# Retention and SiLU feed-forward on one core: the first two slices of w_in loaded first in 2 KB rows, TensorE given matmuls to do until data lands, the early order rewritten

## The chip, the cores and the metric

The kernel runs on one core of a Trainium2 chip. The metric is the device time of one execution in microseconds, lower being better. The version before has a median of 623.32 us over four runs (620.6 to 625.35). The profiled execution is one of them.

## The reference, cut to what matters

The computation has two parts. The first is a decayed linear recurrence over time for 4 batches and 8 heads, with sequence length 768 and head dimension 64. The second is a feed-forward layer with SiLU over the 3072 rows that come out of it.

```python
state = zeros((B, H, D, D))
for t in range(S):
    state = gamma[None, :, None, None] * state + einsum('bhd,bhe->bhde', k[:, :, t], v[:, :, t])
    y[:, :, t] = scale * einsum('bhd,bhde->bhe', q[:, :, t], state)
x = y.transpose(0, 2, 1, 3).reshape(B * S, H * D)      # 3072 x 512
h = x @ w_in                                           # 512 x 2048
out = (h / (1 + exp(-h))) @ w_out                      # 2048 x 512
```

q, k and v arrive as 32-bit floats. The two weight matrices arrive as 64-bit floats.

## The kernel before, in words

**Units.** The sequence is cut into 6 chunks of 128 steps. A unit is one chunk of one batch, so there are 24 units, numbered chunk by chunk; units 0 to 3 are chunk 0. For a unit n, in the names of the order written out at the end of the kernel:

- `T(n)` transposes k and q on TensorE (4 transposes each, L436), and ScalarE copies each result from PSUM (L438). k's result goes to a PSUM bank that `turn` hands out, q's to another.
- `K(n)` scales k by powers of the decay on VectorE (L398); `Q(n)` does it for the transposed q (L403).
- `SC(n)` is 16 matmuls for the new state's sums (L452) and 16 for the scores (L462). `A(n)` has three steps: the mask, which multiplies the scores by the decay on VectorE (L470), then the middle state (L476 on ScalarE in chunk 0, L478 on VectorE later), then the new state (L482).
- `YA(n)` and `YB(n)` multiply the masked scores and the states into y (L501). Between them a one-element memset on GpSimd (L377) keeps two groups of matmuls on PSUM in order.
- `X(n)` has four steps in chunks 0 and 1: ScalarE copies y from PSUM to SBUF (`ys`, L542); ScalarE writes the high part of x (L557); VectorE the low part (L560); VectorE a third part (L563). The parts exist because each feed-forward product is done as three products of a reduced 32-bit float type.

**Slices of w_in.** The feed-forward layer's hidden dimension is cut into 16 slices of 128. `W(i)` does the next of eleven steps that turn slice i's 64-bit words into three parts. In order: 1 absolute value (ScalarE, L196); 2 sign (L199); 3 clamp (L202); 4 shift and join (L206); 5 exponent (L209); 6 low words times a factor (L212); 7 sum (L217), all these on VectorE; 8 high part (ScalarE, L120); 9 remainder (VectorE, L123); 10 middle part (ScalarE, L126); 11 third part (VectorE, L128). A slice is 512 KB, loaded by three DMAs in rows of 1 KB (`load_w`, L178 and L180), into one of two staging buffers.

**Products.** `P(n)` is the first product of 12 matmuls (L650) for one chunk and one slice: eight into `ha`, four into `hb`. The eight need the slice's high and middle parts and x's high and low parts for all four units of the chunk. `CL(n)` closes it in three steps: copy (L660), subtraction on VectorE (L665), SiLU (L670). Results go to memory (`put_g`, L676), and a second half of the kernel multiplies them by w_out (L967).

**Order.** Every engine works through its instructions in the order in which the program issues them. Up to L882 the order of all engines is written out by hand (L768 to L881); later a loop over products runs the rest of the units behind the products. SyncE's queue first takes loads of k, q and v for units 0 to 5 with the first two slices between them (after unit 0 and after unit 3), each load 256 KB in rows of 256 bytes. Then come slice 2 and the loads of further units, in the order of the calls.

The bounds of the parts in the order before: units 0 to 3 run with W(0) and some of W(1) between them; then `P(0)` (L818), unit 4 and the rest of W(1), three steps of W(2), `T(6)`, and `P(1)` (L835).

Of the kernel before, what the change touches and what calls it, by code (L numbers as in the profile page):

```python
# [33 lines left out]
def kernel(  # L34
# [39 lines left out]
    wide = moe_w_in.dtype == mybir.dt.int64  # L74

    scale = 1.0 / math.sqrt(D)
# [8 lines left out]
    wpool = pool("wpool", 1)  # L85
# [3 lines left out]
    one = pool("one", 1)  # L89
    hpool = pool("hpool", 3)  # L90
    stage = pool("stage", 2)
    conv = pool("conv", 1)
# [46 lines left out]
    kqv = {"k": {}, "q": {}, "v": {}}  # L139
    EARLY = 2 * B  # L140
# [21 lines left out]


    staged = {}

    def load_w(i):
        if i >= 2 * NF:
            return
        if wide:
            t = stage.tile([128, 2 * DM], U32, tag="wf", name=f"wf_{i}")  # L170
            w_in, w_out, n = moe_w_in.bitcast(U32), moe_w_out.bitcast(U32), 256
        else:
            t = stage.tile([128, DM], FP32, tag="wf", name=f"wf_{i}")
            w_in, w_out, n = moe_w_in, moe_w_out, 128
        if i < NF:
            to = t.rearrange("p (i o f) -> o p i f", o=2, f=n)
            src = w_in[:, ts(i, n)].rearrange("(i o p) f -> o p i f", o=2, p=128)
            nc.sync.dma_start(out=to[0], in_=src[0])  # L178
            for j in range(2):
                nc.sync.dma_start(out=to[1, ts(j, D)], in_=src[1, ts(1 - j, D)])  # L180
        else:
            nc.sync.dma_start(out=t, in_=w_out[ts(i - NF, 128), :])
        staged[i] = t

    def convert_steps(i, out):

        t = staged.pop(i)
        if not wide:
            out.append(t)
            return  # L190
        words = t.rearrange("p (c w) -> p c w", w=2)
        lo, hi = words[:, :, 0], words[:, :, 1]
        p = a = conv.tile([128, DM], U32, tag="ca", name=f"ca_{i}")
        s = conv.tile([128, DM], U32, tag="cs", name=f"cs_{i}")
        with queue(evac[0] if evac else None):
            nc.scalar.activation(out=a.bitcast(FP32), in_=hi.bitcast(FP32), func=AF.Abs,  # L196
                                 scale=65536.0)
        yield
        nc.vector.tensor_scalar(out=s, in0=hi, scalar1=0x80000000, scalar2=None,  # L199
                                op0=ALU.bitwise_and)  # L200
        yield
        nc.vector.tensor_scalar(out=a.bitcast(FP32), in0=a.bitcast(FP32),  # L202
                                scalar1=bits(1024 << 20), scalar2=bits((1279 << 20) - 1),
                                op0=ALU.max, op1=ALU.min)
        yield
        nc.vector.scalar_tensor_tensor(out=s, in0=a, scalar=3, in1=s,  # L206
                                       op0=ALU.logical_shift_left, op1=ALU.bitwise_or)
        yield
        nc.vector.tensor_scalar(out=p, in0=s, scalar1=0xFF800000, scalar2=None,  # L209
                                op0=ALU.bitwise_and)  # L210
        yield
        nc.vector.scalar_tensor_tensor(out=p.bitcast(FP32), in0=lo, scalar=2.0 ** -52,  # L212
                                       in1=p.bitcast(FP32), op0=ALU.mult, op1=ALU.mult)
        yield
        w = (s.bitcast(FP32) if i < NF else
             conv.tile([128, DM], FP32, tag="cw", name=f"cw_{i}"))
        nc.vector.tensor_tensor(out=w, in0=s.bitcast(FP32), in1=p.bitcast(FP32), op=ALU.add)  # L217
        out.append(w)
# [68 lines left out]
    def begin_w():  # L287
# [10 lines left out]
    early_order.enter_context(tc.manual_schedule(engines={  # L298
        mybir.EngineType.SP, mybir.EngineType.DVE, mybir.EngineType.Activation,
        mybir.EngineType.Pool}))  # L300
    for n in range(EARLY - 2):
        for name in "kqv":
            load(name, n)
        if n in (0, 3):
            load_w(n // 3)


    ident = const.tile([128, 128], FP32, tag="ident", name="ident")
# [10 lines left out]
    for j in range(2):  # L319
        for a in range(HP):  # L320
            nc.scalar.activation(out=decay[:, j, a, :], in_=lag[:, :D], func=AF.Exp,
                                 scale=float(lg[2 * a + j]))
# [40 lines left out]
    def banks(tag, name, n=2):  # L363
        return ps_u.tile([128, n, 512], FP32, tag=tag, name=name)
# [3 lines left out]
    def turn(name):  # L368
        turns[0] += 1
        return ps_h.tile([128, 512], FP32, tag=f"h{turns[0] % 3}", name=name)  # L370
# [55 lines left out]
        nc.scalar.copy(out=to[n].bitcast(U16).rearrange("p a (t w) -> p w a t", w=2),  # L426
                       in_=turned.pop((name, n)).rearrange("p (w a) t -> p w a t", w=2))

    def stage_t(n):

        for name, to, bufs, src, tp in (
                ("kt", kt, 2, kqv["k"][n], turn(f"kp_{n}")),
                ("qt", qt, 3, kqv["q"].pop(n), banks("q", f"qp_{n}", 1)[:, 0])):
            tp = tp.rearrange("p (a t) -> p a t", a=HP)
            for a in range(HP):
                nc.tensor.transpose(tp[:, a, :], src[:, 2 * a : 2 * a + 2, :], ident)  # L436
            to[n] = one.tile([128, HP, C], FP32, tag=name, name=f"{name}_{n}", bufs=bufs)
            evac[:] = [nc.scalar.copy(out=to[n], in_=tp).ins]  # L438

    def score_tile(n):  # L440
        u = banks("s", f"sc_{n}")
# [85 lines left out]
    def finish_y(n, yp):  # L527
        list(steps_y(n, yp))

    raws = []  # L530

    def steps_y(n, yp):
        c, b = units[n]
        if b == 0:
            p, tag = (wpool, "wq") if c == LATE else (xpool, "xt")
            xt[c] = p.tile([128, 3, KIN, NT], FP32R, tag=tag, name=f"xt_{c}")
        raw = None
        if c < LATE:
            if n == 0:
                raws.append(wpool.tile([128, LATE * B, KIN, C], FP32, tag="wq", name="ys"))  # L540
            raw = raws[0][:, n]
            nc.scalar.copy(out=raw.rearrange("p a (o t) -> p o a t", o=2), in_=yp)  # L542
        elif c == LATE:
            raw = hpool.tile([128, KIN, C], FP32, tag="hs", name=f"ys_{n}")
            nc.scalar.copy(out=raw.rearrange("p a (o t) -> p o a t", o=2), in_=yp)
            nc.sync.dma_start(out=y_dram[b], in_=raw)
        yield from split_x(c, b, yp, raw)
# [125 lines left out]
    def put_g(keep):  # L673
        while len(pending) > keep:
            c, f, g = pending.pop(0)
            nc.sync.dma_start(out=g_dram[c, f], in_=g)  # L676
# [50 lines left out]

    sa, ys, asteps, ysteps = {}, {}, {}, {}

    def T(n):  # L730
        stage_t(n)

    def SC(n):
        sa[n] = sc, sums = score_tile(n)
        stage_s(n, sums)
        stage_a(n, sc)
        asteps[n] = steps_a(n, sc, sums)

    def A(n):
        next(asteps[n], None)  # L740

    def YA(n):
        ys[n] = stage_y(n)
# [12 lines left out]
    def W(i, times=1):  # L756
        if i not in slices:
            slices[i] = early_slice(i)
        for _ in range(times):
            next(slices[i], None)  # L760

    def loads(n):
        for name in "kqv":
            load(name, n)

    K, Q = scale_k, scale_q

    T(0), K(0)  # L768
    nc.scalar.activation(out=token, in_=lgc[:1, :1], func=AF.Silu)
    SC(0), A(0), Q(0), A(0), A(0)  # L770
    W(0), W(0), W(0), W(0), W(0)
    YA(0), YB(0), X(0)
    T(1), K(1)
    W(0)
    load_w(2)
    W(0)
    X(0), X(0)
    SC(1), A(1)
    W(0)
    A(1)  # L780
    Q(1), A(1)
    T(2), K(2)
    W(0), X(0)
    W(0), W(0)
    YA(1), SC(2)
    A(2)
    YB(1), X(1)
    A(2), Q(2), A(2)
    X(1)
    T(3), K(3)  # L790
    X(1), X(1)
    YA(2), YB(2), X(2)
    SC(3), A(3), A(3), Q(3), A(3)
    X(2), W(1), W(1)
    X(2), X(2)
    YA(3), YB(3), X(3), X(3)
    W(1), W(1)
    T(4)
    X(3), X(3)
    K(4)  # L800
    W(1), W(1)
    loads(EARLY - 2), loads(EARLY - 1)
    closing = {}

    def P(n):
        c, f = divmod(n, NF)
        closing[n] = close_steps(c, f, *multiply(c, f))

    def CL(f):
        next(closing[f], None)  # L810

    def KA(n):
        t = kqv["k"][n]
        for h in range(H):
            nc.scalar.activation(out=t[:, h, :], in_=t[:, h, :], func=AF.Copy,
                                 scale=gk[:, units[n][0], h : h + 1])

    P(0)  # L818
    next_chunk()
    SC(4)  # L820
    CL(0), CL(0), CL(0)
    put_g(0)
    W(1)
    T(5)
    A(4), A(4), Q(4), K(5), A(4)
    W(1), W(1)
    YA(4), SC(5), YB(4)
    loads(EARLY)
    load_w(3)
    W(2), W(1)  # L830
    A(5)
    W(1), W(2), W(2)
    X(4)
    T(6)
    P(1)  # L835
    A(5), Q(5), A(5)
    KA(6)
    W(2), W(2), W(2)
    load("k", EARLY + 1), load("q", EARLY + 1)
    load_w(4)  # L840
    W(2)
    CL(1), CL(1)
# [184 lines left out]
```

## Time and profile before

| | us |
|---|---|
| median of four runs | 623.32 |
| the profiled execution, whole | 622.53 |
| its span, first to last instruction | 620.7 |
| TensorE busy (matmul rows) | 601.8 |
| VectorE busy | 423.4 |
| ScalarE busy | 312.7 |

The time of a run is the span and some 1.8 us around it. Times of instructions are counted from the span's start. In the profile a 32-bit float matmul has two rows, one for each pass: the scores are 384 matmuls and have 768 rows; a transpose has one row. "Granted clock" is the share of full speed that TensorE's clock gate gave.

The beginning is where the change is:

| stretch, us | TensorE busy | VectorE busy | ScalarE busy | DMA, GB/s |
|---|---|---|---|---|
| 0 to 5 | 0.80 | 0.00 | 3.96 | 137 |
| 5 to 10 | 4.05 | 2.10 | 3.84 | 239 |
| 10 to 15 | 3.38 | 4.90 | 2.98 | 200 |
| 15 to 20 | 3.67 | 4.79 | 3.72 | 212 |
| 20 to 25 | 3.45 | 3.15 | 2.26 | 195 |
| 25 to 30 | 2.91 | 3.87 | 3.14 | 216 |
| 30 to 35 | 5.00 | 3.37 | 2.04 | 227 |
| 35 to 40 | 4.24 | 4.28 | 4.04 | 254 |

### The profile page before, as it was taken

Reading aid. Unit: us, or ns where it says so; the run is one execution under the profiler, and the core shown is the slowest. Engines: PE = TensorE matmul, PEld = TensorE weight load, DVE = VectorE, ACT = ScalarE, POOL = GpSimd, SP = SyncE. Lnnn points to the kernel's source line nnn. Section 1 sums busy time; section 2 is a strip of 40 time slices with the busy share of each in tenths; the row PEclk is TensorE's granted clock in tenths of the full one; section 3 lists DMA queues with packets and bytes.
Section 4 is the critical chain, followed back from the end, with each engine's and each line's share of the span. In section 5 each row is a group of like instructions: output and inputs, shape, how many; then the busy total and the mean of one; then the engine's idle time right before and its main releaser. Section 6 shows DMA issues by size and latency. Waiting matters only on the chain.

```text
span 620.7 us, 13494 instructions
## 1 busy us (share of the span) xinstructions
PE 601.8 (97%) x5384; PEld 496.1 (80%) x5384; DVE 423.4 (68%) x731; ACT 312.7 (50%) x595; POOL 22.5 (4%) x79
## 2 busy tenths in 40 slices
PE   5799999999999999999999999999999999999997
PEld 4577787888888888888788888888888888888886
DVE  4889899898889877767599783644635454554631
ACT  7668797666655666666588741412222221412311
POOL 3000000000001211111000000000000000000000
PEclk9999999999999999999999999999999999999999
DMA  9998896555567899989767552432523433442301
GB/s 189 218 224 193 217 243 205 178 171 194 201 159 234 242 253 227 259 223 295 260 220 255 203 150 72 149 123 75 187 79 120 152 101 103 136 135 83 122 1 68
DMA packets 137998, 107.31 MB, mean 173 GB/s; under 512 B 94800, under 2 KB 103248, under 8 KB 137936
## 3 DMA queue, kind: packets, MB, share of 16 engines
q1 hardware_dynamic: 135056, 101.21, 57.7%
q10 hardware_dynamic: 2880, 5.24, 2.3%
q8 instruction: 42, 0.69, 0.5%
q14 instruction: 20, 0.16, 0.1%
HBM read 66.06 MB, written 36.70 MB: 166 GB/s over the span
## 4 chain that ended last, share of the span: by engine, by line
PE 83%; DVE 0%; DVEq 0%; issue 0%; POOLq 0%
PE ha L650 25%; PE o L967 21%; PE oa L967 14%; PE hb L650 12%; PE ob L967 7%; PE y L501 2%; PE sc L462 1%; PE sc L452 1%; PE o L975 0%; PE oa L975 0%; PE qp L436 0%; PE kp L436 0%; PE ob L975 0%; DVE o L993 0%; DVEq L1022 0%
## 5 line engine op out<-in xcount | busy, mean ns | idle before, releaser
L650 PE MATMUL ha<-xt,wi 128*128 128x512 f32 x768 | 195.2, 396 | 1.1 <-ACT xt L557 0.7
L650 PEld LDWEIGHTS ha<-xt,wi 128*128 128x128 f32 x768 | 143.0, 189 | 33.3 <-ACT wi L126 1.2
L967 PE MATMUL o<-wo,gs 128*128 128x512 f32 x564 | 143.2, 389 | 0.0
L717 DVE TENSOR_TENSOR gs<-gr,gs 128x512 fp32r<-128x512 f32 x96 | 62.3, 686 | 90.2 <-ACT gs L715 90.2
L967 PEld LDWEIGHTS o<-wo,gs 128*128 128x128 f32 x564 | 105.9, 188 | 21.8
L715 ACT ACTIVATE gs<-gr 128x512 fp32r<-128x512 f32 x96 | 53.6, 621 | 134.2 <-issue 131.8
L967 PE MATMUL oa<-wo,gs 128*128 128x512 f32 x376 | 115.9, 390 | 0.0
L650 PE MATMUL hb<-xt,wi 128*128 128x512 f32 x384 | 102.9, 390 | 0.7 <-DVE g L665 0.7
L665 DVE TENSOR_TENSOR g<-g,hb 128x512 f32<-128x512 f32 x96 | 65.8, 685 | 43.6 <-ACT g L660 25.0
L650 PEld LDWEIGHTS hb<-xt,wi 128*128 128x128 f32 x384 | 72.1, 188 | 16.1 <-DVE g L665 1.1
L670 ACT ACTIVATE g<-g 128x512 f32<-128x512 f32 x96 | 60.3, 628 | 46.9 <-DVE g L665 46.8
L967 PEld LDWEIGHTS oa<-wo,gs 128*128 128x128 f32 x376 | 70.6, 188 | 14.8
L967 PE MATMUL ob<-wo,gs 128*128 128x512 f32 x188 | 73.8, 392 | 0.0
L660 ACT ACTIVATE g<-ha 128x512 f32<-128x512 f32 x96 | 57.0, 593 | 31.9 <-PE ha L650 18.2
L718 DVE SCALAR_TENSOR_TENSOR gs<-gs 128x512 fp32r<-128x512 f32 x96 | 62.1, 685 | 0.0
L967 PEld LDWEIGHTS ob<-wo,gs 128*128 128x128 f32 x188 | 35.3, 188 | 8.6 <-DVE o L985 1.6
L196 ACT ACTIVATE ca<-wf 128x512 f32<-128x512 f32 x32 | 21.4, 667 | 7.0 <-DVE cw L217 5.8
L212 DVE SCALAR_TENSOR_TENSOR ca<-wf,ca 128x512 f32<-128x512 uint32 x32 | 22.8, 711 | 0.5
L984 ACT ACTIVATE o<-o 128x512 f32<-128x512 f32 x10 | 6.0, 599 | 33.4 <-PE o L967 33.0
L206 DVE SCALAR_TENSOR_TENSOR cs<-ca,cs 128x512 uint32<-128x512 uint32 x32 | 22.1, 692 | 0.9
L470 DVE TENSOR_TENSOR am<-sc,decay 128x512 f32<-128x512 f32 x24 | 16.5, 688 | 8.3 <-PE sc L462 8.2
L501 PE MATMUL y<-qt,mid 64*64 64x64 f32 x384 | 19.7, 220 | 2.3 <-issue 1.8
(93 smaller groups left out, 556.6 us busy)
## 6 DMA issues: line engine op xcount, KB each, us to landing
gd<-g SPq DMA_DIRECT2D x96, 256.0 KB, 3.2
gr<-gd SPq DMA_DIRECT2D x96, 256.0 KB, 2.7
wf<-in_moe_w_out_dram SPq DMA_DIRECT2D x16, 512.0 KB, 4.4
out_dram<-o ACTq DMA_DIRECT2D x20, 256.0 KB, 2.1
wf<-in_moe_w_in_dram SPq DMA_DIRECT2D x16, 256.0 KB, 4.0
wf<-in_moe_w_in_dram SPq DMA_DIRECT2D x32, 128.0 KB, 3.9
kf<-in_k_dram SPq DMA_DIRECT2D x16, 256.0 KB, 5.2
qf<-in_q_dram SPq DMA_DIRECT2D x16, 256.0 KB, 4.3
```

The source lines that it names most:

```text
L196: nc.scalar.activation(out=a.bitcast(FP32), in_=hi.bitcast(FP32), func=AF.Abs, scale=65536.0)
L206: nc.vector.scalar_tensor_tensor(out=s, in0=a, scalar=3, in1=s, op0=ALU.logical_shift_left, op1=ALU.bitwise_or)
L212: nc.vector.scalar_tensor_tensor(out=p.bitcast(FP32), in0=lo, scalar=2.0 ** -52, in1=p.bitcast(FP32), op0=ALU.mult, op1=ALU.mult)
L501: i = nc.tensor.matmul(yp[ts(e, D), o, a, :], lhsT=lhsT, rhs=rhs, start=(e, o) not in started, stop=True, skip_group_check=True).ins
L650: nc.tensor.matmul(hb if i == 2 else ha, lhsT=w_sb[f][:, i, ts(kk, 128)], rhs=xt[c][:, i, kk, :], start=kk == 0 and i != 1, stop=kk == KIN ...
L660: copied[:] = [nc.scalar.activation(out=hs, in_=ha, func=AF.Copy, scale=ONE_E).ins]
L665: taken_out[:] = [nc.vector.tensor_tensor(out=hs, in0=hs, in1=hb, op=ALU.subtract).ins]
L670: nc.scalar.activation(out=hs, in_=hs, func=AF.Silu)
L715: nc.scalar.activation(out=t[:, 0, :], in_=g, func=AF.Copy, scale=HALF)
L717: nc.vector.tensor_tensor(out=t[:, 1, :], in0=g, in1=high, op=ALU.subtract)
L718: nc.vector.scalar_tensor_tensor(out=t[:, 2, :], in0=t[:, 1, :].bitcast(FP32), scalar=-1.0 / EPS, in1=high, op0=ALU.mult, op1=ALU.add)
L967: nc.tensor.matmul(o, lhsT=g, rhs=wo[f][:, i, :], start=f == 0 and i != 1, stop=f == NF - 1 and i != 0)
```

## The change

Four things are edited.

1. **Loads.** A new function `load_pair` loads slices 0 and 1 together, ahead of all loads of k, q and v, in three DMAs (512 KB and twice 256 KB) whose rows are 2 KB. They land in a tile `room` that takes the place of the tile `ys` in the same memory. Slice 0's two scratch tiles lie in `room` as well, so W(0) and W(1) no longer share scratch. The bytes are the same. Slice 2 no longer waits for a staging buffer. The loads of k and q for unit 9 are issued ahead of slice 3 in place of behind it.
2. **x of units 0 to 3.** Their y is no longer copied to SBUF: the high part (ScalarE) and the low part (VectorE) of x are read from PSUM. The first step of `X(n)` does nothing for these units. Units 4 to 7 keep the copy.
3. **TensorE.** A new function `keep_busy` issues 22 matmuls of the identity by itself ahead of `T(0)`.
4. **The order by hand** up to `P(1)`: the steps of W(0) and W(1) begin ahead of unit 0; `T(n)` of units 1 to 4 is cut into its k and its q half with `YA` between; masks stand ahead of the x steps of the unit before; `SC(4)` stands ahead of `P(0)`. From `P(1)` on the order of compute is unchanged.

```diff
+    room = [wpool.tile([128, 12 * DM], U32, tag="wq", name="room")]
+
+    def load_pair():
+        ...
+        t = room[0][:, 8 * DM :].rearrange("p (r f) -> p r f", f=2 * 256)
+        to = t.rearrange("p (i o) f -> o p i f", o=2)
+        src = moe_w_in.bitcast(U32)[:, : 2 * 256].rearrange("(i o p) f -> o p i f", o=2, p=128)
+        nc.sync.dma_start(out=to[0], in_=src[0])
+        for j in range(2):
+            nc.sync.dma_start(out=to[1, ts(j, D)], in_=src[1, ts(1 - j, D)])
+        for i in range(2):
+            staged[i] = t[:, :, ts(i, 256)]
...
+    load_pair()
     for n in range(EARLY - 2):
         for name in "kqv":
             load(name, n)
-        if n in (0, 3):
-            load_w(n // 3)
...
+    def keep_busy(n, t=None):
+        t = turn(f"none_{turns[0]}") if t is None else t
+        for _ in range(n):
+            nc.tensor.matmul(t[:, :128], lhsT=ident, rhs=ident, start=True, stop=True)
+        return t
...
-        if c < LATE:
-            if n == 0:
-                raws.append(wpool.tile([128, LATE * B, KIN, C], FP32, tag="wq", name="ys"))
-            raw = raws[0][:, n]
+        if B <= n < LATE * B:
+            raw = room[0][:, ts(n - B, DM)].bitcast(FP32).rearrange("p (a t) -> p a t", a=KIN)
             nc.scalar.copy(out=raw.rearrange("p a (o t) -> p o a t", o=2), in_=yp)
...
+    keep_busy(22)
+    nc.scalar.activation(out=token, in_=lgc[:1, :1], func=AF.Silu)
+    W(0, 2), W(1, 2)
+    W(0, 3)
+    load_w(2)
     T(0), K(0)
...
+    W(0, 3), W(1)
+    SC(0)
     W(0)
+    A(0), A(0), Q(0), A(0)
+    T(1, "k"), K(1)
+    W(0)
+    YA(0), T(1, "q"), YB(0)
     W(0)
     X(0), X(0)
+    SC(1)
+    X(0), W(1)
+    A(1), A(1), Q(1)
+    T(2, "k")
+    A(1), K(2), X(0)
+    YA(1), T(2, "q"), YB(1), X(1), X(1)
+    SC(2)
+    X(1), W(1)
+    A(2), A(2), Q(2)
+    T(3, "k")
+    A(2), K(3), X(1)
+    YA(2), T(3, "q"), YB(2), X(2), X(2)
+    SC(3)
+    X(2)
+    A(3), A(3), Q(3)
+    T(4, "k")
+    A(3), K(4), X(2)
+    YA(3), T(4, "q"), YB(3), X(3), X(3)
+    SC(4)
+    X(3)
+    A(4), X(3)
     loads(EARLY - 2), loads(EARLY - 1)
...
+    next_chunk()
     P(0)
-    next_chunk()
-    SC(4)
-    CL(0), CL(0), CL(0)
+    A(4), Q(4), A(4)
+    W(1)
+    CL(0)
+    T(5)
+    CL(0), CL(0)
     put_g(0)
+    W(1, 2)
+    K(5)
+    YA(4), SC(5), YB(4)
+    W(1, 2)
+    A(5)
     W(1)
-    T(5)
-    A(4), A(4), Q(4), K(5), A(4)
-    W(1), W(1)
-    YA(4), SC(5), YB(4)
     loads(EARLY)
+    load("k", EARLY + 1), load("q", EARLY + 1)
     load_w(3)
-    W(2), W(1)
-    A(5)
-    W(1), W(2), W(2)
+    W(2, 3)
     X(4)
     T(6)
     P(1)
```

More of the change, by code (lines that the diff above doesn't have):

```diff
@@ L164 @@
     staged = {}
+    room = [wpool.tile([128, 12 * DM], U32, tag="wq", name="room")]
+    def load_pair():
+        if not wide:
+            load_w(0), load_w(1)
+            return
+        t = room[0][:, 8 * DM :].rearrange("p (r f) -> p r f", f=2 * 256)
[6 more added lines that the diff above has]
+            staged[i] = t[:, :, ts(i, 256)]
     def load_w(i):
@@ L190, in convert_steps, with by_rows @@
             return
[L191 to L194, printed above, removed]
+        if len(t.shape) == 2:
+            t = t.rearrange("p (r f) -> p r f", r=KIN)
+        words = t.rearrange("p r (c w) -> p r c w", w=2)
+        lo, hi = words[:, :, :, 0], words[:, :, :, 1]
+        def by_rows(x):
+            return x.rearrange("p (r c) -> p r c", r=KIN)
+        if i == 0:
+            p = a = room[0][:, ts(4, DM)]
+            s = room[0][:, ts(5, DM)]
+        else:
+            p = a = conv.tile([128, DM], U32, tag="ca", name=f"ca_{i}")
+            s = conv.tile([128, DM], U32, tag="cs", name=f"cs_{i}")
         with queue(evac[0] if evac else None):
-            nc.scalar.activation(out=a.bitcast(FP32), in_=hi.bitcast(FP32), func=AF.Abs,
-                                 scale=65536.0)
+            nc.scalar.activation(out=by_rows(a.bitcast(FP32)), in_=hi.bitcast(FP32),
+                                 func=AF.Abs, scale=65536.0)
         yield
-        nc.vector.tensor_scalar(out=s, in0=hi, scalar1=0x80000000, scalar2=None,
+        nc.vector.tensor_scalar(out=by_rows(s), in0=hi, scalar1=0x80000000, scalar2=None,
                                 op0=ALU.bitwise_and)
@@ L211, in convert_steps @@
         yield
-        nc.vector.scalar_tensor_tensor(out=p.bitcast(FP32), in0=lo, scalar=2.0 ** -52,
-                                       in1=p.bitcast(FP32), op0=ALU.mult, op1=ALU.mult)
+        nc.vector.scalar_tensor_tensor(out=by_rows(p.bitcast(FP32)), in0=lo,
+                                       scalar=2.0 ** -52, in1=by_rows(p.bitcast(FP32)),
+                                       op0=ALU.mult, op1=ALU.mult)
         yield
@@ L427, in join_t, with stage_t @@
                        in_=turned.pop((name, n)).rearrange("p (w a) t -> p w a t", w=2))
[L429 to L433, printed above, removed]
+    def stage_t(n, names="kq"):
+        for name in names:
+            if name == "k":
+                to, bufs, src, tp = kt, 2, kqv["k"][n], turn(f"kp_{n}")
+            else:
+                to, bufs, src, tp = qt, 3, kqv["q"].pop(n), banks("q", f"qp_{n}", 1)[:, 0]
             tp = tp.rearrange("p (a t) -> p a t", a=HP)
@@ L436, in stage_t @@
                 nc.tensor.transpose(tp[:, a, :], src[:, 2 * a : 2 * a + 2, :], ident)
-            to[n] = one.tile([128, HP, C], FP32, tag=name, name=f"{name}_{n}", bufs=bufs)
+            to[n] = one.tile([128, HP, C], FP32, tag=f"{name}t", name=f"{name}t_{n}", bufs=bufs)
             evac[:] = [nc.scalar.copy(out=to[n], in_=tp).ins]
+    def keep_busy(n, t=None):
[3 more added lines that the diff above has]
+        return t
     def score_tile(n):
@@ L528, in finish_y @@
         list(steps_y(n, yp))
-    raws = []
     def steps_y(n, yp):
@@ L728, with T @@
     sa, ys, asteps, ysteps = {}, {}, {}, {}
-    def T(n):
-        stage_t(n)
+    def T(n, names="kq"):
+        stage_t(n, names)
     def SC(n):
@@ L766 @@
     K, Q = scale_k, scale_q
-    T(0), K(0)
[L769 to L773, printed above, removed]
-    W(0)
-    load_w(2)
+    keep_busy(22)
[3 more added lines that the diff above has]
+    load_w(2)
+    T(0), K(0)
+    W(0, 3), W(1)
+    SC(0)
+    W(0)
+    A(0), A(0), Q(0), A(0)
+    T(1, "k"), K(1)
+    W(0)
+    YA(0), T(1, "q"), YB(0)
     W(0)
     X(0), X(0)
[L778 to L796, printed above, removed]
-    W(1), W(1)
[L798 to L801, printed above, removed]
+    SC(1)
[19 more added lines that the diff above has]
+    A(4), X(3)
     loads(EARLY - 2), loads(EARLY - 1)
@@ L816, in KA @@
                                  scale=gk[:, units[n][0], h : h + 1])
+    next_chunk()
     P(0)
-    next_chunk()
-    SC(4)
-    CL(0), CL(0), CL(0)
-    put_g(0)
-    W(1)
-    T(5)
-    A(4), A(4), Q(4), K(5), A(4)
-    W(1), W(1)
-    YA(4), SC(5), YB(4)
+    A(4), Q(4), A(4)
[3 more added lines that the diff above has]
+    CL(0), CL(0)
+    put_g(0)
+    W(1, 2)
[3 more added lines that the diff above has]
+    A(5)
+    W(1)
     loads(EARLY)
+    load("k", EARLY + 1), load("q", EARLY + 1)
     load_w(3)
-    W(2), W(1)
-    A(5)
-    W(1), W(2), W(2)
+    W(2, 3)
     X(4)
@@ L838 @@
     W(2), W(2), W(2)
-    load("k", EARLY + 1), load("q", EARLY + 1)
     load_w(4)
```

## The prediction, made before the change had run

> **What bounds the kernel now.** I read first the page's busy shares and the chain of work that ended last, then that chain in order of time.
>
> ```profile
> PE 601.8 (97%) x5384; PEld 496.1 (80%) x5384; DVE 423.4 (68%) x731; ACT 312.7 (50%) x595; POOL 22.5 (4%) x79
> ...
> PE 83%; DVE 0%; DVEq 0%; issue 0%; POOLq 0%
> ...
> 100.26 0.04 issue
> 100.31 1.20 PE ha L650 x4
> ```
>
> From 100.3 us to the end the chain is TensorE alone. The change can only bring that stretch forward: before 100 us TensorE is busy 85.3 us (sum of the windows), so 14.7 us are idle there, nearly all before 60 us. Next, windows; the columns are busy time of PE, PEld, DVE, ACT and POOL, then granted clock, DMA share and GB/s.
>
> ```profile
> 21.95:25.36 3.41, 2.31 (x112) 2.06 (x112) 1.84 (x5) 1.81 (x4) 0.04 (x1) 1.00 1.20 231
> 25.36:28.78 3.42, 1.51 (x17) 1.33 (x17) 2.32 (x5) 1.56 (x4) 0.04 (x1) 0.98 0.92 198
> 28.78:32.19 3.41, 3.41 (x8) 2.71 (x9) 2.95 (x5) 2.04 (x6) 0.00 (x0) 0.52 0.91 242
> ...
> 38.48:63.51 25.03, 23.60 (x528) 19.16 (x519) 23.48 (x44) 19.80 (x50) 0.35 (x4) 1.00 0.87 206
> ```
>
> From 38.48, where unit 5's mask starts, VectorE is busy 23.48 of 25.03 us. Its order from there on is nearly the same after the change, so **what counts is when unit 5's mask starts** (38.48 now): whatever it gains or loses is carried into the TensorE-bound part. The VectorE and TensorE timelines show what delays it:
>
> ```profile
> 8.49 0.69 DVE L470 TENSOR_TENSOR am<-sc,decay 128x512 f32<-128x512 f32 x1 [2.41 <-PE sc L462]
> ...
> 23.41 0.69 DVE L470 TENSOR_TENSOR am<-sc,decay 128x512 f32<-128x512 f32 x1 [1.71 <-PE sc L462]
> ...
> 33.40 0.69 DVE L665 TENSOR_TENSOR g<-g,hb 128x512 f32<-128x512 f32 x1 [1.60 <-PE hb L650]
> ...
> 38.48 0.69 DVE L470 TENSOR_TENSOR am<-sc,decay 128x512 f32<-128x512 f32 x1 [0.72 <-PE sc L462]
> ```
>
> ```profile
> 20.06 0.68 PE L501 MATMUL y<-am,kqv 64*64 64x64 f32 x26
> 21.10 0.34 PE L501 MATMUL y<-am,kqv 64*64 64x64 f32 x6 [0.36 <-issue]
> ...
> 26.95 0.45 PE L501 MATMUL y<-qt,mid 64*64 64x64 f32 x8 [1.77 <-issue]
> ...
> 28.74 3.63 PE L650 MATMUL ha<-xt,wi 128*128 128x512 f32 x8 [0.32 <-ACT xt L557]
> ```
>
> VectorE starves behind TensorE. TensorE has three troubles: late data, stalls that wait for nothing shown ("issue"), and a halved clock in P(0).
>
> **The stalls are instruction fetch.** Counting matmul rows in program order (T 8, SC 64, YA 40, YB 8 for a unit of chunk 0), the stalls at 21.10 and 25.46 to 26.95 fall at rows 346 and 473: 127 apart, with their weight loads some 256 instructions. The DMA view shows one 16 KB packet of the instruction queue from 12.4, 18.6, 23.8, 29.2 and 37.8 us, each 2 to 3 us after TensorE passes row 92, 219, 346, 473 or 600:
>
> ```profile
> q8 instruction: 1, 0.02, 41.2%
> ```
>
> That is the one of 12.4 to 12.6: 41.2% of 16 engines for 0.2 us is 1.32 us on one of them. So passing one edge fetches the block behind the next. Row 219 passes at 16.45, 346 at 21.10, 473 at 26.95: **4.65 and 5.85 us per block of 127 rows, mean 5.25**.
>
> **The change, part by part.**
>
> **Loads.** Issue plus time to landing, per DMA: k0 4.05, q0 5.3, v0 6.4, slice 0 8.7, k1 9.8, q2 15.6, q3 19.4, v3 21.5, slice 1 24.1, v4 27.4. A k, q or v takes 1.2 us each undisturbed and (21.5 - 9.8)/8 = 1.46 us on the average; slices take 2.3 and 2.6. Both first: the link effectively starts at 4.05 - 1.2 = 2.85, so the pair lands at 2.85 + 4.9 = 7.75 at the rate of 1 KB rows, or at 6.35 at the 303 GB/s of the fastest early microsecond; 2 KB rows have no row here. I take 6.6, nearer the fast end since rows are longer. Then k0 7.8, q0 9.0, v0 10.2, k1 11.4, and at 1.46: v1 14.3, v2 18.7, v3 23.1, v4 27.4. Unit 0 gets its data 3.8 us later, unit 4 at the same time. Slice 0 is 2.1 us and slice 1 17.5 us earlier. The k and q moved past slice 3 are needed at 55; slice 3 at 59.6: nothing.
>
> **VectorE and ScalarE.** Up to unit 5's mask VectorE issues about 31 instructions of 512 elements at a 0.60 us pitch and 18 short ones at 0.34: 25 us. From 6.6 that fits by 31.6, so VectorE no longer decides unless TensorE is much faster. Four copies of 0.59 us (L542) go; ScalarE is not the bound here: nothing. Instead low parts are read from PSUM (0.69, by L470 and L665, which read PSUM and take the same) and hold y's bank some 1.3 us longer; the next YA comes a mask later: nothing, or 0.6 us per unit if masks come early. Silu's table load (1.28) moves behind gq, 5.5 to 6.8, under the pair's transfer; it can hold slice 0's first step by 0.4 us.
>
> **keep_busy.** 22 f32 matmuls are 44 rows; nearest are the k transposes of the same shape: cold 4 in 1.09 us, pitch 0.21, later 4 in 0.66, pitch 0.13. From 1.4 us (identity ready at 1.31): 16 cold rows to 4.9, where the clock would open, 28 at 0.13: done at 8.5; if it opens only at 8.3, at 9.8. So T(0) starts 0.7 (at most 2.0) after k0, but warm: T(0) and SC(0) take 2.2 us less than the cold 4.2 to 8.43, 0.4 us each for four groups being the visible part. I take SC(0) at 10.3 to 11.5, against 6.5 to 8.4.
>
> **The TensorE chain with fetch.** Rows in the new order: SC(0) ends at 116, SC(1) 236, SC(2) 356, SC(3) 476, SC(4) 596, P(0) 608, SC(5) 728; each 44 later for the keep_busy, and P(0) also 64 for SC(4). Row 92 passes at 10.9, so 219 (in SC(1), data at 14.3) opens at 16.15, 346 (in SC(2)) at 21.4, 473 (end of SC(3)) at 26.65, 600 at 31.9. After 473: mask and T(4) of k to 27.5, YA(3) 28.4, T(4) of q 29.0, YB(3) 29.4, SC(4) 30.6, P(0) 30.7 to 34.1 with 0.6 lost at row 600. T(5) 1.1, YA(4) 0.9: SC(5) starts 36.1, and unit 5's mask 1.2 later (as now): **37.4, a gain of 1.1 us**. P(0) starts 2 us later than now, but at full clock and with unit 4's scores done.
>
> **Two rules against the rows.** Row: stalls of 0.4 and 1.5 us at block edges. The Trainium skill, "Runtime: NRT & Kernel Launch", Instruction fetch mechanics, says that crossing a 16 KiB boundary is "mostly hidden". By it nothing but data decides: SC(4) at v4, P(0) at 28.5, T(5) 31.5, unit 5's mask at 34.8, a gain of 3.7. I keep the row. Row: the clock halved at 28.78 after a window with 1.51 of 3.42 us busy and no gap over 1.77; 1.98 busy (11.71 to 15.12) didn't halve it. The skill's "TensorE: Matmul & The Clock Gate", Part 1, puts the fall after at least one idle window, which by its text would never come here. By the row I expect about 2.1 busy in that window after the change: kept, though barely; if not, P(0) loses 1.6 us as now (3.63 + 1.09 against 2.09 + 1.07 for P(1)).
>
> **Sum.** Against this execution: 622.5 - 1.1 = **621.4 us**. It stands 0.8 below the median of 623.3. A difference under 0.5% (3.1 us) can't be told from none.
>
> **Rivals.**
> - **Fetch hides, or is quick (30%).** For: the stalls come only with fully loaded queues, at 33 to 39 us there are none. Against: the load is the same. At 4.65 us per block the mask starts near 36.0: 620.0; all hidden: 618.8.
> - **Slower: unit 0's lateness is not made up (20%).** Its place is SC(0), 3.8 us later, with 44 rows more ahead of each SC. For: blocks at 5.85 us give edges 16.75, 22.6, 28.45, 34.3, P(0) at 32.5 to 36.3, mask at 40.2: a loss of 1.7; the window to 28.78 is then nearly idle, the clock halves, 1.0 more: 625.2. It decides once a block takes over 5.5 us. Against: only one did.
> - **It does not do what it says (5%).** keep_busy leaves a gap to k0, the clock falls again, and SC(0) runs cold: 0.9 later, about 622.3.
>
> The forecast holds 45%. Range 617.8 to 625.6: both first rivals' ends with 1 us below and 0.4 above. Faster by over 0.5% needs most of the hidden fetch or a gain I have not found: 0.31; slower by as much needs more than the slow rival: 0.18; else 0.51.
>
> **What would show it.** Right: the pair landed by 6.6; SC(0) near 10.3 and warm; "issue" stalls in SC(1) to SC(3) at 127-row distances; P(0) 30 to 31 at clock 1.0; unit 5's mask near 37.4. Wrong: no such stalls; P(0) before 28.7; clock 0.5 in P(0); VectorE idle between 40 and 63.

## The result, and the profile after

The changed kernel takes **623.73 us** (median of 35 runs, 621.62 to 628.18), the kernel before 623.03 in the runs beside it. The ratio is 1.0018, 95% interval 1.0005 to 1.0031: slower by about a fifth of a per cent, where 621.4 had been forecast. The profiled execution took 623.75 us with a span of 621.9, against 622.53 and 620.7 before.

The busy shares and the chain of work that ended last:

```profile
PE 607.3 (98%) x5428; PEld 501.3 (81%) x5428; DVE 423.2 (68%) x731; ACT 310.8 (50%) x591; POOL 22.0 (4%) x79
...
PE 83%; issue 0%; DVE 0%; DVEq 0%; POOLq 0%
```

The chain still ends in a long TensorE stretch. TensorE is busy 5.5 us more: the 44 rows of keep_busy take 7.8, and P(0) at full clock takes less. The only difference in its list is that "issue" now stands second. Next, the windows that answer to those of before (busy time of PE, PEld, DVE, ACT and POOL, then granted clock, DMA share and GB/s), and VectorE's and TensorE's timelines of the early part:

```profile
21.90:25.30 3.40, 3.16 (x96) 2.58 (x96) 3.11 (x7) 1.50 (x4) 0.09 (x1) 1.00 0.74 168
25.30:28.70 3.40, 2.45 (x87) 1.87 (x80) 2.24 (x5) 1.30 (x3) 0.00 (x0) 1.00 0.82 184
28.70:32.10 3.40, 3.40 (x83) 2.90 (x84) 2.80 (x5) 2.25 (x6) 0.09 (x1) 1.00 0.94 231
37.24:62.27 25.03, 23.14 (x528) 18.90 (x529) 23.38 (x44) 20.90 (x52) 0.35 (x4) 1.00 0.91 216
```

```profile
7.86 0.43 DVE L222 TENSOR_SCALAR room<-room 128x512 uint32<-128x512 uint32 x1 [7.86 <-DMA room<-in_moe_w_in_dram]
...
37.24 0.69 DVE L501 TENSOR_TENSOR am<-sc,decay 128x512 f32<-128x512 f32 x1 [0.27 <-PE sc L493]
```

```profile
1.37 7.80 PE L468 MATMUL none<-ident 128*128 128x128 f32 x44 [1.37 <-POOL ident masks.py:199]
...
11.23 0.69 PE L483 MATMUL sc<-kqv 64*64 64x64 f32 x32 [0.65 <-DMA kqv<-in_v_dram]
...
21.94 0.34 PE L493 MATMUL sc<-qt,kt 64*64 64x64 f32 x8 [0.41 <-issue]
26.74 0.21 PE L493 MATMUL sc<-qt,kt 64*64 64x64 f32 x1 [0.75 <-issue]
30.55 2.12 PE L677 MATMUL ha<-xt,wi 128*128 128x512 f32 x8
```

So far the forecast holds in the main: SC(0) at 11.23 and warm, stalls in SC(2) and SC(3) at rows 348 and 475 (127 apart), P(0) at 30.55 with the clock at 1.00, unit 5's mask at 37.24. (The stall forecast in SC(1) did not come.) The mask is 1.24 us earlier than in the trace of before. Followed on, that lead is 0.85 us at VectorE's tenth subtraction of `CL`, which closes a product; here it is in the change, then before:

```profile
87.28 0.68 DVE L692 TENSOR_TENSOR g<-g,hb 128x512 f32<-128x512 f32 x1
```

```profile
88.13 0.68 DVE L665 TENSOR_TENSOR g<-g,hb 128x512 f32<-128x512 f32 x1
```

The lead is still 0.82 at 192 us, and a loss of 1.2 at the end. TensorE's timeline of the change between 190 and 204 us shows where it turns:

```profile
192.35 0.96 PE L677 MATMUL ha<-xt,wi 128*128 128x512 f32 x3
193.66 1.43 PE L677 MATMUL ha<-xt,wi 128*128 128x512 f32 x5 [0.35 <-issue]
...
199.86 0.63 PE L493 MATMUL sc<-qt,kt 64*64 64x64 f32 x26
201.43 0.28 PE L493 MATMUL sc<-qt,kt 64*64 64x64 f32 x3 [0.94 <-issue]
```

The same two places in the trace of before:

```profile
193.17 2.11 PE L650 MATMUL ha<-xt,wi 128*128 128x512 f32 x8
...
200.05 0.65 PE L462 MATMUL sc<-qt,kt 64*64 64x64 f32 x32
```

Eight matmuls of ha lasted 2.11 us and now reach from 192.35 to 195.09: 0.63 more. The 32 scores lasted 0.65 and now reach from 199.86 to past 201.7: about 1.26 more. Counted in program order the stalls stand at rows 2631 and 2758, again 127 apart. Each ends soon after a 16 KB packet of the instruction queue has come in. One starts at 191.30 us and takes 0.88, the next starts at 198.58 and takes 1.45; TensorE goes on 1.48 and 1.40 us after their ends. The DMA view of the change from 198.5 to 198.7 us shows the second (45.4% of 16 engines for 0.2 us is 1.45 us on one):

```profile
q8 instruction: 1, 0.02, 45.4%
```

They are stalls for instruction blocks inside the part that is TensorE alone, where nothing makes them up. 1.9 us lost there turn a lead of 0.82 into a lag of 1.07.

### The profile page after: what moved, and what is told of

It is laid out like the page before. It is cut to its first block, busy times and chain, and to the rows that moved or that the text cites. A ratio compares the mean times of both kernels' runs of the same rounds, so it can differ in the third digit from the quotient of the medians.

```text
span 621.9 us, 13575 instructions
## 1 busy us (share of the span) xinstructions
PE 607.3 (98%) x5428; PEld 501.3 (81%) x5428; DVE 423.2 (68%) x731; ACT 310.8 (50%) x591; POOL 22.0 (4%) x79
## 4 chain that ended last, share of the span: by engine, by line
PE 83%; issue 0%; DVE 0%; DVEq 0%; POOLq 0%
PE ha L677 25%; PE o L998 21%; PE oa L998 14%; PE hb L677 12%; PE ob L998 7%; PE y L532 2%; PE sc L493 1%; PE sc L483 1%; PE o L1006 0%; PE oa L1006 0%; PE kp L461 0%; PE qp L461 0%; PE ob L1006 0%; DVE o L1024 0%; DVEq L1053 0%
## 5 line engine op out<-in xcount | busy, mean ns | idle before, releaser
L219 ACT ACTIVATE ca<-wf 128x512 f32<-128x512 f32 x30 | 20.0, 668 | 6.8 <-DVE cw L241 6.4
L235 DVE SCALAR_TENSOR_TENSOR ca<-wf,ca 128x512 f32<-128x512 uint32 x30 | 21.4, 714 | 0.4
L1016 DVE TENSOR_TENSOR o<-o,o 128x512 f32<-128x512 f32 x10 | 6.8, 688 | 19.3 <-ACT o L1015 19.3
L532 PE MATMUL y<-qt,mid 64*64 64x64 f32 x384 | 19.7, 220 | 0.0
```

The costliest lines, as they stand in the source:

```text
L219: nc.scalar.activation(out=by_rows(a.bitcast(FP32)), in_=hi.bitcast(FP32), func=AF.Abs, scale=65536.0)
L235: nc.vector.scalar_tensor_tensor(out=by_rows(p.bitcast(FP32)), in0=lo, scalar=2.0 ** -52, in1=by_rows(p.bitcast(FP32)), op0=ALU.mult, op1= ...
L532: i = nc.tensor.matmul(yp[ts(e, D), o, a, :], lhsT=lhsT, rhs=rhs, start=(e, o) not in started, stop=True, skip_group_check=True).ins
```

## The experiments

**Theories.** A: the 44 rows moved every later block edge, some of them to places where TensorE stalls, and the stalls took the gain. B (rival, and what the expectations below call B): the late loss comes from something else in the change, such as the loads, the places in memory or the time that the large keep_busy takes. C (rival): the beginning gained nothing in the first place, and 38.48 was one bad execution. The added matmuls below write scratch space that nothing reads.

Three numbers are read from each trace: the start of unit 5's mask; the time from there to the tenth subtraction of `CL`; and the time from that subtraction to the end, nearly all TensorE-bound. Before: 38.48, 49.65, 532.60. After: 37.24, 50.04, 534.64. Ratios are to the kernel before on the same chip; a trace is one execution, and need not be a typical one.

**No keep_busy** (the row count of before):

```diff
-    keep_busy(22)
```

> The change without its 22 early matmuls (44 matmul rows fewer on TensorE from the start on). Theory A, instruction fetch: the 44 rows moved the edges of TensorE's 16 KB instruction blocks, so that two edges fell into the bursts at 193 and 201 us and cost 0.6 and 1.3 us there. Without them the edges lie as before the change: no 'issue' stall of TensorE between 60 and 300 us, the gain of 0.8 us at 190 us (less what a cold TensorE costs in T(0) and SC(0), up to 0.9) is kept to the end: ratio 0.998 to 1.000. Theory B, the late loss comes from the other order of loads or the other places in memory: the two late losses stay, ratio 1.002 or more.

Measured: **1.0071** [1.0047, 1.0094]; mask at 43.16, to the end 533.05. No "issue" wait between 188 and 320 us, as A wants. But the beginning is 6 us later than in the change. (The traced execution, 629.75 us, was the longest of 13; their median is 625.74.) TensorE's timeline, then the windows, of this kernel:

```profile
20.47 0.34 PE L532 MATMUL y<-am,kqv 64*64 64x64 f32 x7 [0.76 <-issue]
...
34.30 0.27 PE L532 MATMUL y<-qt,mid 64*64 64x64 f32 x2 [1.03 <-issue]
...
61.15 0.35 PE L493 MATMUL sc<-qt,kt 64*64 64x64 f32 x8 [2.53 <-issue]
```

```profile
20.87:24.28 3.41, 3.41 (x83) 2.96 (x78) 1.06 (x3) 1.18 (x2) 0.09 (x1) 0.50 0.97 219
24.28:27.70 3.42, 1.46 (x44) 1.03 (x40) 2.84 (x6) 0.86 (x2) 0.00 (x0) 1.00 0.71 151
27.70:31.11 3.41, 3.41 (x72) 2.96 (x74) 0.39 (x1) 1.18 (x2) 0.09 (x1) 0.50 0.96 237
```

The edges now stop TensorE at other instructions. Three windows run at half the clock, from 20.87, 27.70 and 61.83 us: the first and the third follow such a stop, the second a wait of 1.72 us for VectorE. The order of loads is that of the change, yet the beginning is worse than in any trace of before.

**Small matmuls in place of the large ones**, 22, 15 or 33 of them (64 x 64, two rows each):

```diff
+    def small(n):
+        t = turn(f"small_{turns[0]}")
+        for _ in range(n):
+            nc.tensor.matmul(t[:D, :D], lhsT=ident[:D, :D], rhs=ident[:D, :D], start=True, stop=True)
...
-    keep_busy(22)
+    small(22)
```

> The change with the 22 early matmuls made 64 by 64 in place of 128 by 128: the same 44 rows and instructions, but done some 4 us sooner. Theory A: the stalls near 193 and 201 us stay, as the count of instructions is the same; ratio 1.001 to 1.003. If it is the time of the 22 matmuls that matters (a warm clock or T(0) started late) and not their count: the late stalls go or the beginning differs by over 1 us.

> The change with 15 small matmuls (30 rows) at the start in place of its 22. Against 22 small ones only the count differs: the block edges come 14 rows later everywhere. By the rows' times in the trace with 22 small ones, that leaves no pair of edges under 4.6 us apart after 40 us (with 22: 2.7 us apart at 190 us, 3.6 us at 225 us). Theory A (edges that fall into one burst): no 'issue' stall over 0.5 us after 40 us, ratio 0.998 to 1.000. If stalls come by chance, or the loss is in the new order itself: 1.001 to 1.003.

> The same with 33 small matmuls (66 rows, edges 22 rows sooner than with 22). One pair of edges is 3.0 us apart, at 48 to 51 us; none later under 4.6 us. Theory A: a stall of 0.5 to 1.5 us near 51 us, none after 60 us: ratio 1.000 to 1.002. Otherwise 1.001 to 1.003 with late stalls.

Measured: 1.0021 [1.0004, 1.0038], 1.0015 [1.0005, 1.0025] and 1.0015 [0.9998, 1.0032]; masks at 37.10, 37.30 and 37.96; to the end 533.93, 535.03 and 533.69. With 22 the beginning and the total are those of the change: it makes no difference here that the large matmuls take 7.8 us, and what the two kernels share is the number of instructions. The other two were to slide the edges out of the bursts. They only slid along:

```profile
200.01 0.21 PE L538 MATMUL y<-qt,state 64*64 64x64 f32 x1 [1.15 <-issue]
```

```profile
192.65 0.27 PE L499 MATMUL sc<-qt,kt 64*64 64x64 f32 x2 [0.83 <-issue]
```

The first is TensorE's timeline with 15, the second with 33. Both counts missed: a unit's visit is 128 to 136 small rows, longer than a block, so some edge lies in it whatever the shift.

**A whole block of rows**, keep_busy(22) and small(42), 128 rows, which puts the late edges back within a row of before's:

```diff
     keep_busy(22)
+    small(42)
```

> The change with 42 small matmuls behind its 22, in all 128 matmul rows ahead of T(0), about one block of instructions: the edges lie nearly as before the change again. Theory A: no 'issue' stall at 193 and 201 us, the early gain kept, less what the 84 small rows take (about 3 to 5 us of TensorE, if they end after k of unit 0 lands up to 2 us of delay of unit 0): ratio 0.997 to 1.000. Theory B: 1.002 or more, with the losses at 193 and 201 us.

Measured: 1.013 [1.0099, 1.0161]; mask at 44.41, to the end 532.89 with no late stall. The tail went back to before's, as A says. The beginning lost 7.2 us: the small ones run to 13.8, so T(0) is 4.7 us later, and stalls of 0.73 at 24.77 and 1.08 at 35.56 and the halved clock from 19.7 come on top.

**The rows alone, on the kernel before**: 22 small matmuls ahead of T(0), or ahead of the third product, 55 us in, where the early part is over:

```diff
+    small(22)
     T(0), K(0)
```

```diff
+    filler(22)   # small matmuls into a bank of "q"
     P(NF)
```

> The kernel before with nothing but 22 small matmuls (44 rows) ahead of T(0), done by about 4 us, when k of unit 0 lands. Theory A: the edges lie as in the change, so TensorE stalls near 193 to 194 and 200 to 202 us for 0.5 to 1.3 us each: ratio 1.002 to 1.003, less what a warmer TensorE brings at the start. Theory B: no such stalls, ratio 0.999 to 1.001.

> The kernel before, its beginning untouched, with 22 small matmuls (44 rows) put on TensorE only at about 61 us, ahead of the third product, where TensorE waits 0.7 us for VectorE soon after. Theory A (instruction-block edges): from there on the edges lie as in the change, so TensorE stalls at about 193 and 201 us by 0.6 and 1.3 us; with 0.7 us of filler that stays visible, 2.0 to 2.8 us longer than before: ratio 1.003 to 1.0045. Theory B (the late loss comes from something else in the change): only the filler, at most 0.7 us, ratio 1.000 to 1.001, no 'issue' stall near 193 and 201 us.

> The 22 small matmuls at 60 us in the kernel before once more, on the same chip as the control: ratio 1.005 to 1.007 again, with a stall near row 2757 (about 200 us) by theory A; without block edges no such stall and the control's ratio.

Measured: 1.0076 [1.005, 1.0101] ahead of T(0); 1.0061 [1.0044, 1.0078] and, repeated, 1.007 [1.0049, 1.0092] later on. The added matmuls take 1.5 us after a wait of 1.33 in the second place; TensorE's timeline of the first version, and then of the second, has what else came:

```profile
196.28 1.89 PE L656 MATMUL ha<-xt,wi 128*128 128x512 f32 x7 [0.56 <-issue]
...
204.76 0.29 PE L468 MATMUL sc<-qt,kt 64*64 64x64 f32 x5 [1.30 <-issue]
```

```profile
201.87 0.28 PE L470 MATMUL sc<-qt,kt 64*64 64x64 f32 x4 [1.00 <-issue]
```

Nothing of the change is in these kernels but the number of instructions, and the late stalls are there, at rows 2629, 2756 and 2757. They are a part of the loss only. With the rows ahead of T(0) the beginning suffered too: T(0) started at 6.25 in place of 4.20, P(0) ran at half the clock, and unit 5's mask came at 41.26. In the later place the rows and the wait before them take 2.8 us of TensorE.

**Control: the time without the rows.** Two long matmuls (four rows) in the same place, behind the same wait, move the edges by four rows only:

```diff
+    filler(2)   # lhsT=ident, rhs=decay (128 x 512)
     P(NF)
```

> Control for the 22 small matmuls at 60 us in the kernel before: at the same place 2 long ones (4 rows, 512 columns), about 1.7 us of TensorE by two passes of 0.43 us each, against 1.5 us for the 44 short rows. Theory A (block edges): edges move by 4 rows only, no late stall, so it costs its own time alone: ratio 1.001 to 1.003, below that of the 22 small ones by 1 us or more. If the filler's time or place is what costs: the same ratio as the 22 small ones, 1.005 to 1.007.

Measured: 1.0035 [1.0017, 1.0054], to the end 532.99, no late stall. In the trace the two matmuls hold TensorE for 3.66 us, as the granted clock was at 0.50 from 55.40 to 58.81; at full clock they would take about 1.7 us, by the estimate just quoted, against 1.5 us for the 44 rows. With no less TensorE time added than in the version before it, the control loses half as much. The difference, 0.26 to 0.35% or 1.6 to 2.2 us, is what moved edges cost here; but the intervals overlap a little, by 0.10% with the first of the two runs and by 0.05% with the second, so its size is rough. The traces bear the direction out: the tail is 532.99 us here, 533.92 and 533.49 with the 44 rows.

**A second shift on top of the change**: 12 small matmuls (24 rows) ahead of the third product, in the change (twice) and with 22 small ones in place of keep_busy:

```diff
+    filler(12)
     P(NF)
```

> The change with 12 small matmuls (24 rows) put at the same place, about 60 us, nothing else. Theory A: its beginning stays (unit 5's mask some 1.2 us earlier than before), the edges move 24 rows up, out of the start of the bursts: the stalls at 193 and 201 us are gone, 1.9 us less than the change less up to 0.5 us of filler: ratio to before 0.9985 to 1.000. Theory B: the late loss stays, ratio 1.002 to 1.003.

> The change with the 12 small matmuls at 60 us once more: its first trace had no late stall and a span 2.2 us below the change's, but its median did not fall. Theory A in full: again no stall after 70 us, and the median must then fall below the change's by over 1 us. If stalls there come and go from run to run: this trace has some after 70 us, and the median stays at 1.002.

> The change with 22 small matmuls in place of its large ones at the start, and the 12 small ones at 60 us. Theory A: early gain 1.3 us, no stalls at 193 and 201 us: ratio 0.998 to 0.9995, the fastest of this set. Theory B: 1.002.

Measured: 1.0022 [1.0009, 1.0035], 1.0033 [1.0018, 1.0048], 1.0025 [1.0009, 1.004]; to the end 532.56, 534.78, 533.51. The first trace has no late stall and a span of 619.7, but it was among the shortest of its 22 runs (621.9 against a median of 623.67). The repeat and the third stall again (0.21 us at 192.74, 0.59 at 192.97). Most of the repeat's long tail is something else: 1.5 us of it are lost between 217 and 249 us, where scores wait 0.57 us for ScalarE's copy of k (at 241.08). In all three kernels the time outside the span is also 2.1 us, where the others have 1.8 to 1.9. This was meant to be the cure and is none.

**The pair in 1 KB rows**, one slice after the other, both still first:

```diff
-        nc.sync.dma_start(out=to[0], in_=src[0])
-        for j in range(2):
-            nc.sync.dma_start(out=to[1, ts(j, D)], in_=src[1, ts(1 - j, D)])
+        for i in range(2):
+            cols = ts(i, 256)
+            nc.sync.dma_start(out=to[0][:, :, cols], in_=src[0][:, :, cols])
+            for j in range(2):
+                nc.sync.dma_start(out=to[1, ts(j, D)][:, :, cols], in_=src[1, ts(1 - j, D)][:, :, cols])
```

> The change with the two slices loaded first, but in rows of 1 KB, by six DMAs in place of three; instructions of the compute engines are the same. If 2 KB rows are worth what my prediction took (pair landed by 6.6 in place of 7.75 us), the second slice lands 1 us later than in the change and unit 0's mask moves by as much. If rows of 1 KB are as fast: the pair lands within 0.4 us of the change's, k of unit 0 likewise, ratio 1.001 to 1.003.

> Slices first in 1 KB rows and 15 small matmuls. Theory A: as with 15 small ones, with unit 5's mask up to 1 us sooner: ratio 0.996 to 0.999, faster than both kernels. Otherwise 1.000 to 1.002.

> Slices first in rows of 1 KB, and the 12 small matmuls at 60 us. Theory A: the early gain of the 1 KB version (unit 5's mask 2.5 us earlier than before) and no late stalls: ratio 0.996 to 0.999. If late stalls are chance: ratio 1.000 to 1.002.

Measured: 1.001 [0.9996, 1.0025]; with 15 small ones for keep_busy 1.0022 [1.0008, 1.0036]; with the second shift 1.0027 [1.0011, 1.0042]. VectorE's timeline of the first:

```profile
7.17 0.43 DVE L224 TENSOR_SCALAR room<-room 128x512 uint32<-128x512 uint32 x1 [7.17 <-DMA room<-in_moe_w_in_dram]
...
35.95 0.69 DVE L503 TENSOR_TENSOR am<-sc,decay 128x512 f32<-128x512 f32 x1 [0.25 <-PE sc L495]
```

VectorE's first step on the pair stands at 7.17 here and at 7.70 and 8.05 in the other two kernels with 1 KB rows; in the ten traces with 2 KB rows it stands between 7.58 and 8.35. So the long rows bring nothing here. The mask came at 35.95, 36.78 and 36.82. Late stalls (0.93 and 0.39 in the first) took it back; the best of this family can't be told from the kernel before, and none beats it.

**Repeats**, to see what a single trace is worth: the kernel before twice, the change once.

> The kernel before once more, as a second trace of it. If its executions differ in where TensorE stalls, the first trace is one draw of several: then this trace shows other 'issue' stalls, above all before 60 us, and a span that differs by up to 2 us. If the stalls are fixed by the program alone, both traces agree within 0.3 us at every mask. The ratio must lie at 1.000 within its interval.

> A third trace of the kernel before. The first two had unit 5's mask at 38.5 and 36.0 us, apart by a fetch stall and a halved clock in the first. If the first was the unusual one, this one lies within 0.7 us of 36.0, with no halved clock in the first product; if the second was, near 38.5. After unit 5's mask it stays parallel to both, with no late stall. Ratio 1.000 within its interval.

> The change once more. Theory A (instruction-block edges in the bursts at 193 and 201 us): the stalls there come again at the same matmul rows (about 2631 and 2758), their lengths may differ; unit 5's mask again 1 to 2.5 us earlier than in the first trace of before. Ratio 1.001 to 1.003. If they are chance: no such stall in this trace.

Measured: 1.0 [0.9984, 1.0016] and 0.9998 [0.9984, 1.0012]; the change 1.003 [1.0016, 1.0045]. The mask of the kernel before came at 36.00 and 35.49. VectorE's and TensorE's timelines of the second repeat:

```profile
35.49 0.69 DVE L470 TENSOR_TENSOR am<-sc,decay 128x512 f32<-128x512 f32 x1 [0.72 <-PE sc L462]
```

```profile
27.28 2.11 PE L650 MATMUL ha<-xt,wi 128*128 128x512 f32 x8 [0.31 <-ACT xt L557]
```

P(0) took 2.11 us there, not 3.63. The halved clock and the stall of 1.77 in the prediction's trace are not in every execution: of six traces with this beginning, two have them, the prediction's and one of the kernel with 22 late matmuls (2.05 us at the same row, P(0) in 3.68). The repeat of the change has its mask at 37.08 and a new loss, in TensorE's timeline and the windows around it:

```profile
54.40 0.80 PE L483 MATMUL sc<-vf,kf 64*64 64x64 f32 x19 [1.83 <-issue]
```

```profile
50.00:53.64 3.64, 2.10 (x67) 1.65 (x66) 3.61 (x8) 3.48 (x9) 0.09 (x1) 1.00 1.11 265
53.64:60.47 6.83, 6.07 (x82) 5.47 (x82) 4.56 (x9) 3.85 (x12) 0.00 (x0) 0.50 0.93 215
```

That is the edge at row 1108, which cost 0.22 us in the change's first trace; with the halved clock after it, the stretch from mask to tenth subtraction is 52.87 us against 50.04. The version in 1 KB rows with the second shift met the same edge (1.10 us, 53.67).

**All twenty traces together.** Six kernels or repeats keep the late edges where before has them, within four rows (before three times, no keep_busy, the whole block, the control): none has an "issue" wait between 188 and 320 us, and the tail takes 532.3 to 533.05 us, mean 532.8. Fourteen have them elsewhere: twelve have such a wait, and the tail takes 532.6 to 535.0, mean 534.0. **With moved edges the TensorE-bound part is 1.2 us longer on the average.** The place of the loss points to the edges too. Counted from the tenth subtraction, the 41st, at about 179 us, comes at the same time in all twenty traces within 0.1 us. At the 51st, at about 217 us, the fourteen are 1.0 us behind the six on the average (from 0.2 ahead to 2.1 behind), while the six lie within 0.25 us of their mean.

TensorE has 56 "issue" waits of 0.15 us or more in the twenty traces. Every one stands within three rows of the series 92, 219, 346 and so on in steps of 127, and every one ends 1.2 to 1.75 us after a 16 KB instruction packet has come in, one that started only after TensorE had passed the edge before. **So the "issue" waits are waits for instructions.** They are not common: 56 of 833 edges from row 219 on.

How fast TensorE uses up a block does not decide alone which edge stalls. Before's three traces passed the block that ends at row 3267 in 2.7 to 3.1 us without a stall. In the change TensorE had 6.5 us from row 2631 until it stopped at row 2758; there the packet started late, 4.6 and 5.0 us after the edge before it in the two traces.

The beginning of before, untouched in six traces (before three times, the control, and the late rows twice), puts unit 5's mask at 35.49 to 39.58, mean 37.15; that of the change, in four (the change and late12, twice each), at 36.81 to 37.24, mean 37.09. **The beginning is steadier and not earlier**: it is ahead of the two traces with the halved clock in P(0) (38.48 and 39.58), and no earlier than the other four (35.49 to 37.03, mean 36.2).

## Why the prediction was wrong

**The step that failed** is the one that ties the beginning to the end: "Its order from there on is nearly the same after the change", and "whatever it gains or loses is carried into the TensorE-bound part". The order is the same, its place in the instruction blocks is not. The working counted the 44 rows only for edges up to row 600. The edges at rows 2631 and 2758 then fell on other instructions, where the next block was not there in time; the working had put their price at nothing. In the first trace these stalls cost 1.9 us against a gain of 0.85; over the fourteen traces with moved edges, 1.0 us on the average between 179 and 217 us. The theory (A) is shown by the rows alone on the kernel before, by the tail that comes back with a whole block of rows, and by the packets at the stalls; the control agrees, within its wide interval.

**The baseline** was a second failure (C). The mask was forecast at 37.4 and came at 37.24 and 37.08, so that sum was right, but the 1.1 us of gain were counted from 38.48, one execution with a long stall. Against the mean of 37.15 there was no gain to carry. No gain in the beginning and 1.2 us lost in the tail are near the 1.1 and 1.9 us that the two ratios of the change amount to. The edge at row 1108, which cost 0.22 us in one trace of the change and 1.83 with a halved clock in the other, is a third part that two traces can't weigh. That 623.73 lies inside the stated range is owed to the range's width; the direction was wrong.

**Term by term.**
- Loads: the pair was to be landed at 6.6, and VectorE's first step on it stands at 7.86. The slow bound, 7.75 by the rate of 1 KB rows, was nearer; preferring the fast end "since rows are longer" was wrong, as 7.17 to 8.05 with 1 KB rows show.
- keep_busy: T(0) was to start at 8.5 and starts at 9.01; SC(0) at 11.23 lies within 10.3 to 11.5. The rows' pitch fell at 6.90 us, later than the 4.9 taken. keep_busy had no price beyond that, and none for its rows at the late edges.
- Fetch: 127 rows a block, stalls expected up to the end of SC(3): found at 21.94 and 26.74 (forecast 21.4 and 26.65). The one forecast at 16.15 and the 0.6 us at row 600 did not come. (In the prediction's trace the long stall began at 25.18 by its 1.77 us, not at 25.46; nothing rests on it.) The Trainium skill ("Runtime: NRT & Kernel Launch", Instruction fetch mechanics) calls the crossing "mostly hidden". For 777 of 833 edges that holds here; the other 56 cost 0.2 to 2.5 us each. The row was rightly kept, and then not applied far enough.
- Clock: the window from 25.30 was to have about 2.1 us busy and stay at full clock; it had 2.45, and P(0) ran in 2.12. The skill's "TensorE: Matmul & The Clock Gate", Part 1, wants at least one idle window before a fall. Here it fell after partly busy windows, with up to 1.87 of 3.41 us busy, so the measured row was the better rule.
- Rivals: the slower one, unit 0's lateness, did not come (P(0) at 30.55, not 32.5). Slowness came by a mechanism in none of the three. That all fetch hides is excluded by the 56 stalls.

**What stays open.** The medians of the shifted change (late12, twice) did not fall even though one of its traces shows no late stall, so the split of the median's loss between the early edges, row 1108 and the late ones is not settled. Why a packet starts 0.1 us after an edge in one place and 5 us after it in another, and why the same block is late in one execution and in time in the next, was not tried by itself; load on the DMA queues is likely, and only argued.

## What to carry to other kernels

Where TensorE runs bursts of small matmuls, every instruction added ahead moves all later block edges. Count them to the end of the program: the count says where a stall can come, not whether it will. Judge such a change by a control that adds the same time in few instructions. Before a stall in one trace is taken as the gain to be had, take two or three traces of the same kernel; here the baseline's mask moved by 3 us (35.49 to 38.48). A lead won before a long bound stretch is worth only what that stretch doesn't lose again.

## What the runs showed of the hardware

- Passing a block edge costs nothing or up to 2.53 us, and differs between executions: row 1108 cost 0.22 us in one trace of the change and 1.83 in the other; the row 473 of before cost 1.77 us in one of its three traces and nothing in the others.
- One packet of 16 KB on the instruction queue (0.9 to 1.6 us on one of the 16 DMA engines in nine of ten cases) feeds some 127 rows, which TensorE used up in as little as 2.2 us. Every one of the 56 stalls ended 1.2 to 1.75 us after such a packet had come in.
- The granted clock fell to 0.50 in 13 places of the twenty traces between 11 and 62 us, for 3.41 us in nine and 6.83 in four. In the 3.41 us before these falls TensorE was busy for 0.89 to 1.87 us. Cut into windows of 3.41 us on the times at which the clock changes, the traces show no window with under 1.84 us busy after which it stayed up, once it had opened, and none with 1.96 or more after which it fell; between 1.84 and 1.87 both came.
- Rows of 2 KB instead of 1 KB made the first two slices no earlier (first use at 7.58 to 8.35 us in ten traces, against 7.17, 7.70 and 8.05).
